# Norms of the first group in two parts of its tokens, U loaded by SP, and the first piece of w1 issued earlier

## The chip, the cores and the metric

The kernel runs on one core of a Trainium2 chip. The metric is the device time of one execution in microseconds. Runs of the same kernel are compared by their medians.

## The reference, cut to what matters

Attention with normalized queries and keys comes first, and a mixer with a two-layer network on its output second. There are 8 batches, 12 heads, 448 tokens and 64 columns a head, so the model width is 768; U is 448 x 32, V is 32 x 448, w_ch1 is 768 x 3072 and w_ch2 is 3072 x 768.

```python
def rmsnorm(x, g):
    return x / np.sqrt(np.mean(x * x, axis=-1, keepdims=True) + 1e-06) * g
q_n, k_n = rmsnorm(q, g_q), rmsnorm(k, g_k)
scores = q_n @ k_n.transpose(0, 1, 3, 2) / 8
attn = softmax(scores)
x = (attn @ v)                      # heads side by side: 8 x 448 x 768
u = x + (x.transpose(0, 2, 1) @ U @ V).transpose(0, 2, 1)
out = u + np.maximum(u @ w_ch1, 0.0) @ w_ch2
```

## The kernel before

**Groups and pairs.** The heads are worked in groups of four, three groups a batch, 24 in all, numbered gi. A group's q, k and v lie in SBUF in float32 tiles (`qf`, `kf`, `vf`, three buffers each). A partition of `qf` holds seven tokens (j) of two heads (c), 14 blocks of 64 columns. A group has two pairs of heads; a pair is scored at once, with `kz` as the stationary operand, which holds the two heads' keys with zeros beside them.

**A group's way.** `squares` (L122 to 130) squares q or k on ACT or POOL; `sums` (L133) adds each block on DVE; `roots` (L139, L140) makes 1/rms on ACT with Ln and Exp; `scale` (L143) multiplies by it on POOL or DVE and writes bf16 (`qn`, `kp`); `turn` (L311) transposes seven blocks on PE; `take_q` (L318 or L320) copies q out of PSUM and multiplies by the product of gains `gg`, on ACT or DVE; `take_k` (L326 to L328) copies k into `kz` on DVE. `values` (L170, L172) casts v on POOL into `va` and `vl`. Then `Sc` (L365, L366) does the scores of a pair in four rounds: two matmuls (one in the last round) and one exponential on ACT. `V` (L378 to L386) multiplies by the values on PE, and DVE divides and writes the batch's rows `x`. Groups from number 6 on are transposed by DMA instead.

**The gains.** g_q and g_k are loaded into one row (`grow`, tile `ob`); POOL multiplies them (L642); `prep_gains` (L232 to L237) makes a bound for the exponent on DVE and spreads both over the partitions with two PE products into `pg`, and DVE copies that into `gg` (L650). `gg` is needed by `take_q` and, as the bias, by every exponential.

**The mixer and the network.** For batch 0, `mix_t0` (L414 to L418) multiplies x by U (in `Uz`), and `mix` (L424 to L431) by V (in `Vm`, prepared on POOL by `prep_v`, L282 and L284) and adds x; this gives `uT`. `up` (L466, L468) and `down` (L479, L487) are the two layers, with weights `w1b` and `w2b` in bf16, loaded and cast by POOL's DMA queue in four and eight pieces (`load_w1` L247, `load_w2` L255).

**What sets the order.** The order is written by hand, and each engine does its instructions in the order in which the program makes them. Up to the end of batch 0's attention the list `att` holds the rounds of `Sc` and, after each, what the table `extra` names for that pair and round. After that two lists, `att` and `mlp`, are merged by costs and due times. In front of all stand the start: memsets, the loads of groups 0 to 2, the WARM matmuls on an identity (L208) that PE does before its first real work, and the norms of group 0. The last lines ahead of the merge are these:

```python
for i in range(2):
    squares(0, i)
...
sums(0, 0)
roots(0, 0, 1)
scale(0, 0, nc.gpsimd)
sums(0, 1)
roots(0, 1, 2)
pg = prep_gains()
scale(0, 1, nc.vector)
nc.vector.tensor_copy(gg, pg)
```

**Queues.** SP issues nearly all loads (L92 for q and k, L99 and L103 for v in four transfers a group, L274 for V). ACT issues k of group 0 and the two gains (L191). POOL issues U (L266 to L268, cast to bf16 under way) and the weights.

Of the kernel before, what the change touches and what calls it, by code (L numbers as in the profile page):

```python
# [13 lines left out]
ALU = AluOpType  # L14
# [3 lines left out]
WARM = 115  # L18
# [6 lines left out]
def kernel(  # L25
# [67 lines left out]

    def load_v(gi, eng=None):
# [28 lines left out]
    def squares(gi, i, eng=None, sq=None):  # L123
# [3 lines left out]
        if eng is None:  # L127
            nc.scalar.activation(sq, staged[gi][i], AF.Square)  # L128
        else:
            eng.tensor_mul(sq, staged[gi][i], staged[gi][i])  # L130

# [53 lines left out]
    grow = small[0:1, 0:2 * D].rearrange("o (i d) -> o i d", i=2)  # L185
    for gi in range(3):
        stage_tiles(gi)
    load_qk(0, 0)
    load_qk(0, 1, nc.scalar)
# [9 lines left out]

    nc.scalar.preload_act_table_set("natural_log_exp_and_others")  # L200
# [12 lines left out]
    nc.vector.memset(eps, 1e-6)  # L213
    for va, vl in zip(va_bufs, vl_bufs):
# [4 lines left out]
    for t in kz_bufs:  # L219
        for a in range(2):  # L220
            nc.vector.memset(t[D:P, a, :S], 0.0)
            nc.vector.memset(t[0:D, a, S:], 0.0)
# [3 lines left out]
    gp = small[0:1, 2 * D:4 * D + 1]  # L226
    ones = small[0:1, 4 * D + 1:4 * D + 1 + P]
    nc.vector.memset(ones, 1.0)
# [34 lines left out]
    nc.gpsimd.memset(Ub[:, NJ:, :], 0.0)  # L263
    Urows = moe_U.rearrange("(p j) r -> p j r", j=NT)
    for i in range(2):
        nc.gpsimd.dma_start(Ub[i * R:(i + 1) * R, :NJ, :], Urows[:, i * NJ:(i + 1) * NJ, :])  # L266
    nc.gpsimd.dma_start(Ub[R:P, NJ, :], Urows[:, 2 * NJ, :])
    nc.gpsimd.dma_start(Ub[0:R, NJ + 1, :], Urows[:, 2 * NJ, :])  # L268
# [4 lines left out]
    for m in range(NQ):  # L273
        nc.sync.dma_start(Vf[m * rank:(m + 1) * rank, :], moe_V)  # L274
# [12 lines left out]
    first = xp.tile([P, NW, dm], BF16, name="x", tag="x")  # L287
    Uz = first[:, 0, :NW * P].rearrange("p (j r) -> p j r", r=P)
    tz = first[:, 1, :]
    nc.gpsimd.memset(Uz, 0.0)  # L290

    def prep_u():
        nc.vector.tensor_copy(Uz[:, :, :rank], Ub[:, :NW, :])

    tb_bufs = [consts.tile([P, 2 * P], BF16, name=f"tb{i}") for i in range(2)]
    for t in tb_bufs:
        nc.gpsimd.memset(t, 0.0)
# [222 lines left out]
    def turns(gi):  # L520
# [4 lines left out]
        (0, 1): scales(1) + [(0, squares, (2, 1, pool)), (0, keep_busy, (8,))],  # L525
        (0, 2): [(0, keep_busy, (8,))],
        (0, 3): [(0, keep_busy, (8,))],
        (1, 1): [V2(0, 0)],
        (1, 2): [(0, sums, (2, 0))] + turns(1),
        (1, 3): [V2(0, 1), (0, sums, (2, 1)), (0, take_k, (1, 1)), (0, values, (1,)), (0, load, (4,)),  # L530
                 (0, weights, (1,))],
        (2, 1): scales(2) + [(0, weights, (1,)), V2(1, 0)],
# [106 lines left out]
    for i in range(2):  # L639
        squares(0, i)  # L640
    for e in range(2):
# [100 lines left out]
```

## Time and profile before

| what | value |
|---|---|
| median of 3 runs | 606.08 us (605.55 to 606.76) |
| the profiled execution's own time | 602.04 us |
| its span, first to last instruction | 600.3 us |
| busy share: PE, weight loads, DVE, ACT, POOL | 98%, 60%, 34%, 52%, 26% |
| first square of group 0 (ACT) | 5.68 us |
| scaling of q of group 0 (POOL), of k (DVE) | from 8.42, from 9.37 us |
| first exponential | 12.74 us |
| first exponential of group 1, of group 2 | 21.20 us, 29.00 us |
| first w1 issue | 21.67 us |
| first `up` matmul | 41.12 us |

Times inside the execution count from the first instruction. PE, DVE, ACT, POOL and SP are the engines; PEld is PE's loading of stationary operands, beside its matmuls. A line such as L143 is a line of the kernel before. In rows of instructions in order of time, the brackets at the end give how long the engine was idle before and what ended that. POOL's and DVE's instructions are timed one by one; rows with x2 or more merge neighbours of a kind. The granted clock of PE is given as 1.00 throughout.

### The profile page before, as it was taken

The page shows a single profiled execution, that of the slowest core. Times are in us where ns is not written, and L with a number is a line of the kernel's source. Part 1 is how long each engine was busy: PE and PEld are TensorE (multiplying, and loading weights), DVE is VectorE, ACT ScalarE, POOL GpSimd, SP SyncE. Part 2 cuts the span into 40 slices and gives each one's busy share as a digit, 9 for nine tenths or more (in the row PEclk, how much of TensorE's full clock was granted, in tenths as well). Part 3 has the DMA queues.
Part 4 walks back from the last instruction along what each step waited for, and adds up shares of the span by engine and source line. Part 5 has one row for each costly group of instructions (what it writes and reads, how often), then busy time and mean ns, then how long its engine had stood idle before and what let it go on. Part 6 is the DMA issues. An engine that isn't in the chain of part 4 may idle for free.

```text
span 600.3 us, 11625 instructions
## 1 busy us (share of the span) xinstructions
PE 586.2 (98%) x4807; PEld 357.9 (60%) x4807; DVE 206.6 (34%) x474; ACT 312.5 (52%) x479; POOL 158.5 (26%) x271
## 2 busy tenths in 40 slices
PE   8889999999999999999999999999999999999996
PEld 8555656655666556655566655665566655655563
DVE  6686535511343322531235321541234310320011
ACT  6857873477453776356744477346763344004300
POOL 7997633123213303303303312302312000000000
PEclk9999999999999999999999999999999999999999
DMA  9999996784295454675256746277305310230022
GB/s 257 221 243 246 242 199 160 149 204 96 53 206 107 132 124 113 112 179 123 48 134 99 189 116 139 58 174 169 50 2 89 84 27 0 54 72 2 0 54 52
DMA packets 118360, 71.70 MB, mean 119 GB/s; under 512 B 80420, under 2 KB 115108, under 8 KB 118308
## 3 DMA queue, kind: packets, MB, share of 16 engines
q1 hardware_dynamic: 108304, 61.04, 45.0%
q0 software_dynamic: 9728, 9.47, 9.5%
q8 instruction: 37, 0.61, 0.4%
q10 hardware_dynamic: 276, 0.46, 0.2%
q14 instruction: 15, 0.12, 0.1%
HBM read 52.20 MB, written 11.01 MB: 105 GB/s over the span
## 4 chain that ended last, share of the span: by engine, by line
PE 92%; DVE 3%; ACT 2%; DMA 1%; POOL 1%; issue 0%; POOLq 0%; DVEq 0%; ACTq 0%
PE po L479 36%; PE ph L466 35%; PE sc L365 9%; PE pv L382 5%; PE pm L451 2%; PE pv L378 1%; PE busy L208 1%; ACT E L366 1%; DMA qT<-qn 1%; DVE ssq L133 1%; PE pu L399 1%; PE pt L311 1%; DVE x L386 0%; DVE kz L326 0%; POOL sq L130 0%
## 5 line engine op out<-in xcount | busy, mean ns | idle before, releaser
L479 PE MATMUL po<-w2b,hT 128*128 128x384 bf16 x1344 | 241.6, 326 | 1.0 <-DVE x L386 1.0
L466 PE MATMUL ph<-uT,w1b 128*128 128x448 bf16 x1152 | 237.1, 352 | 0.0
L366 ACT ACTIVATE E<-sc,gg 128x896 bf16<-128x896 f32 x192 | 171.9, 911 | 75.3 <-PE sc L365 75.1
L479 PEld LDWEIGHTS <-hT 128*128 128x128 bf16 x1344 | 126.9, 98 | 79.2 <-DVE x L386 1.1
L466 PEld LDWEIGHTS <-w1b 128*128 128x128 bf16 x1152 | 109.7, 98 | 96.1
L468 ACT ACTIVATE hT<-ph 128x448 bf16<-128x448 f32 x192 | 104.0, 545 | 116.7 <-PE ph L466 114.6
L162 POOL TENSOR_TENSOR qn<-qf,rs 128x384 bf16<-128x384 f32 x36 | 29.9, 830 | 279.1 <-ACT rs L140 225.4
L365 PE MATMUL sc<-qT,kz 128*128 128x448 bf16 x336 | 93.7, 352 | 5.2 <-ACT E L366 3.5
L385 DVE RECIPROCAL r<-pv 128x4 f32<-128x4 f32 x96 | 17.4, 181 | 212.2 <-PE pv L382 211.7
L382 PE MATMUL pv<-va,E 128*128 128x65 bf16 x1152 | 57.2, 194 | 0.0
L487 DVE TENSOR_TENSOR ob<-po,x 128x384 f32<-128x384 f32 x48 | 26.8, 558 | 84.6 <-PE po L479 83.4
L382 PEld LDWEIGHTS <-E 128*128 128x128 bf16 x1152 | 50.5, 98 | 7.5
L133 DVE TENSOR_REDUCE ssq<-sq 128x14 f32<-128x896 f32 x47 | 48.8, 1076 | 2.2 <-ACT sq L128 1.7
L365 PEld LDWEIGHTS <-kz 128*128 128x128 bf16 x336 | 31.8, 98 | 29.1 <-issue 4.7
L378 PE MATMUL pv<-vl,E 128*128 128x130 bf16 x192 | 42.1, 219 | 0.0
L386 DVE TENSOR_TENSOR x<-pv,r 128x256 bf16<-128x256 f32 x96 | 40.8, 425 | 3.3
L139 ACT ACTIVATE rs<-ssq,eps 128x28 f32<-128x28 f32 (+1 forms) x25 | 7.9, 318 | 52.4 <-DVE ssq L133 41.1
L456 DVE TENSOR_TENSOR x<-pm,x 128x384 bf16<-128x384 f32 x48 | 26.6, 554 | 17.9 <-PE pm L451 16.8
L162 POOL TENSOR_TENSOR kp<-kf,rs 128x384 bf16<-128x384 f32 x36 | 29.9, 829 | 0.0
L378 PEld LDWEIGHTS <-E 128*128 128x128 bf16 x192 | 18.7, 97 | 8.1 <-issue 1.2
L170 POOL CAST va<-vf 128x768 bf16<-128x768 f32 x24 | 20.7, 863 | 2.0 <-DMA vf<-in_v_dram 2.0
L128 ACT ACTIVATE sq<-qf 128x896 f32<-128x896 f32 x20 | 18.8, 942 | 2.3 <-DMA qf<-in_q_dram 2.3
(84 smaller groups left out, 265.2 us busy)
## 6 DMA issues: line engine op xcount, KB each, us to landing
qf<-in_q_dram SPq DMA_DIRECT2D x24, 448.0 KB, 4.2
kf<-in_k_dram SPq DMA_DIRECT2D x23, 448.0 KB, 5.5
out_dram<-ob SPq DMA_DIRECT2D x50, 192.0 KB, 2.7
vf<-in_v_dram SPq DMA_DIRECT2D x48, 192.0 KB, 5.4
w1b<-in_moe_w_ch_dram POOLq DMA_DIRECT2D x4, 1152.0 KB, 17.1
w2b<-in_moe_w_ch_dram POOLq DMA_DIRECT2D x8, 576.0 KB, 17.5
vf<-in_v_dram SPq DMA_DIRECT2D x48, 32.0 KB, 4.9
out_dram<-ob SPq DMA_DIRECT2D x12, 96.0 KB, 2.5
```

What stands on the lines that cost most here:

```text
L133: nc.vector.tensor_reduce(ssqs[gi][:, i, :], sqs.pop((gi, i)), AX, ALU.add)
L162: nc.gpsimd.tensor_tensor(main.rearrange("p (t i) d -> p i t d", i=2), src[:, c, :2 * NJ].rearrange("p (i t) d -> p i t d", i=2), rs[:, c, ...
L365: nc.tensor.matmul(sc[:, i, :S], kz[:, c:c + P], qT, start=True, stop=True)
L366: nc.scalar.activation(es[(b, pr)][:, 2 * r:2 * r + n, :], sc[:, :n, :S], AF.Exp, scale=scal, bias=bias)
L378: nc.tensor.matmul(pv[:, i].rearrange("p e d -> p (e d)"), E[:, NJ, w:w + P], vl[:, lp, :], start=True, stop=False)
L382: nc.tensor.matmul(pv[:, i, e, :], E[:, e * (NJ + 1) + j, w:w + P], va[:, (lp + 2 * e) * NJ + j, :], start=False, stop=(e == 1 and j == NJ ...
L386: nc.vector.tensor_tensor(xs[b].rearrange("p i (h d) -> p i h d", d=D)[:, 2 * half:2 * half + 2, h0:h0 + 3:2, :], pv[:, :, :, :D], r.rearr ...
L456: nc.vector.tensor_tensor(dst, ph[lo:hi], x[lo:hi], ALU.add)
L466: nc.tensor.matmul(ph, w1b[:, dt, ht * P:(ht + 1) * P], uT[:, dt, off:off + S], start=(dt == 0), stop=(dt == KD - 1))
L468: nc.scalar.activation(hT[:, ht, off:off + S], ph, AF.Relu)
L479: nc.tensor.matmul(po, hT[:, ht, col:col + P], w2b[:, ht, half * HALF:(half + 1) * HALF], start=(ht == 0), stop=(ht == KH - 1))
L487: nc.vector.tensor_tensor(ob[:, h], po, urows(b, col, half), ALU.add)
```

## The change

The loads of q and k of group 0 are split by tokens into j = 0 to 3 and j = 4 to 6, and all four go into SP's queue, q first. Squares, sums and scalings of group 0 are done by the same parts. WARM goes from 115 to 62, and ten more of these matmuls follow the gain products. ACT loads its function table ahead of issuing the gains. The product of the gains stands on POOL ahead of the memset of Vm, and the copy of `gg` stands ahead of k's scaling on DVE. Half of the kz memsets go from DVE to POOL. U is loaded by SP in float32 (into a free part of an x buffer) and cast by DVE in `prep_u`; V is one transfer from a repeated source instead of four. The memsets of Uz and tb go behind the scalings of group 0, and the first piece of w1 is issued right after them; the other pieces of w1 move up by one place. The second square of group 1 goes behind `take_q`, the values of group 0 behind a square of group 2. In `extra`, the scalings of group 1 go one round later, q's turn of group 1 ahead of k's by a round, and the sum of q of group 2 into the start.

```diff
@@ -15,7 +15,7 @@
 
 EXP_ROOM = 80.0
 EXP_SHIFT = 60.0
-WARM = 115
+WARM = 62
 ROWS_FROM = 1
 DMA_FROM = 6
 LEAD = 1.8
@@ -91,6 +91,15 @@
         src = (q, k)[i][b, h0:h0 + n].rearrange("(c a) (p j) d -> (a p) c (j d)", a=2, j=NT)
         (eng or nc.sync).dma_start(staged[gi][i].rearrange("p (c j) d -> p c (j d)", c=2), src)
 
+    def load_qk_part(gi, i, lo, hi):
+
+        b, h0, n = groups[gi]
+        src = (q, k)[i][b, h0:h0 + n].rearrange("(c a) (p j) d -> (a p) c (j d)", a=2, j=NT)[:, :, lo * D:hi * D]
+        nc.sync.dma_start(by_c(staged[gi][i])[:, :, lo:hi, :].rearrange("p c j d -> p c (j d)"), src)
+
+    def by_c(t):
+        return t.rearrange("p (c j) d -> p c j d", c=2)
+
     def load_v(gi, eng=None):
         b, h0, n = groups[gi]
         t = staged[gi][2]
@@ -128,6 +137,22 @@
             nc.scalar.activation(sq, staged[gi][i], AF.Square)
         else:
             eng.tensor_mul(sq, staged[gi][i], staged[gi][i])
+
+
+    def squares_part(i, lo, hi):
+        if (0, i) not in sqs:
+            sqs[(0, i)] = normp.tile([P, 2 * NT, D], FP32, name="sq", tag="sq")
+        nc.scalar.activation(by_c(sqs[(0, i)])[:, :, lo:hi, :], by_c(staged[0][i])[:, :, lo:hi, :], AF.Square)
+
+    def sums_part(i, lo, hi):
+        nc.vector.tensor_reduce(ssqs[0][:, i, :].rearrange("p (c j) -> p c j", c=2)[:, :, lo:hi],
+                                by_c(sqs[(0, i)])[:, :, lo:hi, :], AX, ALU.add)
+
+    def scale_part(i, lo, hi, eng):
+        eng.tensor_tensor(
+            normed[0][i].rearrange("p j c d -> p c j d")[:, :, lo:hi, :], by_c(staged[0][i])[:, :, lo:hi, :],
+            rss[0][:, i].rearrange("p (c j) -> p c j ()", c=2)[:, :, lo:hi, :].to_broadcast([P, 2, hi - lo, D]),
+            ALU.mult)
 
     def sums(gi, i):
         nc.vector.tensor_reduce(ssqs[gi][:, i, :], sqs.pop((gi, i)), AX, ALU.add)
@@ -183,10 +208,15 @@
 
     small = outp.tile([P, dm], FP32, name="ob", tag="ob")
     grow = small[0:1, 0:2 * D].rearrange("o (i d) -> o i d", i=2)
+    gp = small[0:1, 2 * D:4 * D + 1]
+    ones = small[0:1, 4 * D + 1:4 * D + 1 + P]
     for gi in range(3):
         stage_tiles(gi)
-    load_qk(0, 0)
-    load_qk(0, 1, nc.scalar)
+    PARTS = ((0, 4), (4, NT))
+    for i in range(2):
+        for lo, hi in PARTS:
+            load_qk_part(0, i, lo, hi)
+    nc.scalar.preload_act_table_set("natural_log_exp_and_others")
     for i, g in enumerate((g_q, g_k)):
         nc.scalar.dma_start(grow[:, i, :], g.rearrange("(o d) -> o d", o=1))
     for i in range(2):
@@ -197,8 +227,6 @@
     load_v(1)
     load_v(2)
 
-    nc.scalar.preload_act_table_set("natural_log_exp_and_others")
-
     ident = consts.tile([P, P], BF16)
     make_identity(nc, ident)
 
@@ -211,21 +239,21 @@
 
     eps = consts.tile([P, 1], FP32)
     nc.vector.memset(eps, 1e-6)
+    nc.vector.memset(ones, 1.0)
     for va, vl in zip(va_bufs, vl_bufs):
         nc.vector.memset(va[:, :, D:D1], 1.0)
         nc.vector.memset(vl, 0.0)
         for e in range(2):
             nc.vector.memset(vl[e * R:(e + 1) * R, :, e * D1 + D:(e + 1) * D1], 1.0)
-    for t in kz_bufs:
+    for t, eng in zip(kz_bufs, (nc.vector, nc.gpsimd)):
         for a in range(2):
-            nc.vector.memset(t[D:P, a, :S], 0.0)
-            nc.vector.memset(t[0:D, a, S:], 0.0)
+            eng.memset(t[D:P, a, :S], 0.0)
+            eng.memset(t[0:D, a, S:], 0.0)
+    for e in range(2):
+        nc.gpsimd.tensor_mul(gp[:, e * D:(e + 1) * D], grow[:, 0, :], grow[:, 1, :])
 
     gg = consts.tile([P, 2], FP32)
     bias = gg[:, 1:2]
-    gp = small[0:1, 2 * D:4 * D + 1]
-    ones = small[0:1, 4 * D + 1:4 * D + 1 + P]
-    nc.vector.memset(ones, 1.0)
 
     def prep_gains():
         m = gp[:, P:]
@@ -260,18 +288,19 @@
 
 
     Ub = consts.tile([P, NJ + 2, rank], BF16)
-    nc.gpsimd.memset(Ub[:, NJ:, :], 0.0)
+    first = xp.tile([P, NW, dm], BF16, name="x", tag="x")
+    Uf = first[:, 2, :2 * (NJ + 2) * rank].bitcast(FP32).rearrange("p (j r) -> p j r", r=rank)
+    nc.gpsimd.memset(Uf[:, NJ:, :], 0.0)
     Urows = moe_U.rearrange("(p j) r -> p j r", j=NT)
     for i in range(2):
-        nc.gpsimd.dma_start(Ub[i * R:(i + 1) * R, :NJ, :], Urows[:, i * NJ:(i + 1) * NJ, :])
-    nc.gpsimd.dma_start(Ub[R:P, NJ, :], Urows[:, 2 * NJ, :])
-    nc.gpsimd.dma_start(Ub[0:R, NJ + 1, :], Urows[:, 2 * NJ, :])
+        nc.sync.dma_start(Uf[i * R:(i + 1) * R, :NJ, :], Urows[:, i * NJ:(i + 1) * NJ, :])
+    nc.sync.dma_start(Uf[R:P, NJ, :], Urows[:, 2 * NJ, :])
+    nc.sync.dma_start(Uf[0:R, NJ + 1, :], Urows[:, 2 * NJ, :])
 
     NQ = P // rank
     Vf = outp.tile([P, dm], FP32, name="ob", tag="ob")[:, :S]
     Vm = consts.tile([P, NQ, S + R], BF16)
-    for m in range(NQ):
-        nc.sync.dma_start(Vf[m * rank:(m + 1) * rank, :], moe_V)
+    nc.sync.dma_start(Vf, moe_V.rearrange("(m r) s -> m r s", m=1).to_broadcast([NQ, rank, S]))
 
     nc.gpsimd.memset(Vm, 0.0)
 
@@ -284,17 +313,19 @@
             nc.gpsimd.tensor_copy(Vm[r, m, SM:S], cols[:, 2 * NJ])
 
 
-    first = xp.tile([P, NW, dm], BF16, name="x", tag="x")
     Uz = first[:, 0, :NW * P].rearrange("p (j r) -> p j r", r=P)
     tz = first[:, 1, :]
-    nc.gpsimd.memset(Uz, 0.0)
 
     def prep_u():
-        nc.vector.tensor_copy(Uz[:, :, :rank], Ub[:, :NW, :])
+        nc.vector.tensor_copy(Ub, Uf)
+        nc.vector.tensor_copy(Uz[:, :, :rank], Uf[:, :NW, :])
 
     tb_bufs = [consts.tile([P, 2 * P], BF16, name=f"tb{i}") for i in range(2)]
-    for t in tb_bufs:
-        nc.gpsimd.memset(t, 0.0)
+
+    def fill_mixer():
+        nc.gpsimd.memset(Uz, 0.0)
+        for t in tb_bufs:
+            nc.gpsimd.memset(t, 0.0)
 
 
     qk, es, xs = {}, {}, {}
@@ -522,14 +553,14 @@
 
     extra = {
         (0, 0): [(0, keep_busy, (8,))],
-        (0, 1): scales(1) + [(0, squares, (2, 1, pool)), (0, keep_busy, (8,))],
-        (0, 2): [(0, keep_busy, (8,))],
+        (0, 1): [(0, keep_busy, (8,))],
+        (0, 2): scales(1) + [(0, squares, (2, 1, pool)), (0, keep_busy, (8,))],
         (0, 3): [(0, keep_busy, (8,))],
         (1, 1): [V2(0, 0)],
-        (1, 2): [(0, sums, (2, 0))] + turns(1),
-        (1, 3): [V2(0, 1), (0, sums, (2, 1)), (0, take_k, (1, 1)), (0, values, (1,)), (0, load, (4,)),
-                 (0, weights, (1,))],
-        (2, 1): scales(2) + [(0, weights, (1,)), V2(1, 0)],
+        (1, 2): [(0.4, turn, (1, 0)), (0, take_q, (1, 0)), (0, take_q, (1, 1))],
+        (1, 3): [(0.4, turn, (1, 1)), (0, take_k, (1, 0)), V2(0, 1), (0, take_k, (1, 1)), (0, sums, (2, 1)),
+                 (0, values, (1,)), (0, load, (4,)), (0, weights, (1,))],
+        (2, 1): scales(2) + [V2(1, 0)],
         (2, 3): [V2(1, 1)],
         (3, 1): [V2(2, 0)],
         (3, 2): turns(2),
@@ -637,30 +668,37 @@
                 mlp.append((0.98, down, (b, col, half, part, 4), b))
 
     for i in range(2):
-        squares(0, i)
-    for e in range(2):
-        nc.gpsimd.tensor_mul(gp[:, e * D:(e + 1) * D], grow[:, 0, :], grow[:, 1, :])
-    sums(0, 0)
+        for part in PARTS:
+            squares_part(i, *part)
+    for part in PARTS:
+        sums_part(0, *part)
     roots(0, 0, 1)
-    scale(0, 0, nc.gpsimd)
-    sums(0, 1)
+    for part in PARTS:
+        scale_part(0, *part, nc.gpsimd)
+    for part in PARTS:
+        sums_part(1, *part)
     roots(0, 1, 2)
     pg = prep_gains()
-    scale(0, 1, nc.vector)
+    keep_busy(10)
     nc.vector.tensor_copy(gg, pg)
+    for part in PARTS:
+        scale_part(1, *part, nc.vector)
     squares(1, 0)
-    squares(1, 1)
-    values(0)
+    fill_mixer()
+    weights(1)
     squares(2, 0, nc.gpsimd,
             uT.rearrange("p k c -> p (k c)")[:, :4 * NT * D].bitcast(FP32).rearrange("p (j d) -> p j d", d=D))
+    values(0)
     turn(0, 0)
     take_q(0, 0, True)
     take_q(0, 1, True)
+    squares(1, 1)
     turn(0, 1)
     take_k(0, 0)
     sums(1, 0)
     sums(1, 1)
     take_k(0, 1)
+    sums(2, 0)
     load(3)
 
     ia = im = 0
```

## The prediction

> **What bounds the kernel now.** I read the table of stretches first, then the start in order of time on each engine, then the transfers from issue to landing, then the chain that ended last from 28 to 42 us. In the table the columns are length, busy time of PE, its weight loads, DVE, ACT and POOL, granted clock, DMA share and GB/s.
>
> ```profile
> 0.00:12.74 12.74, 10.89 (x139) 10.37 (x140) 8.27 (x33) 6.96 (x11) 8.84 (x19) 1.00 0.92 264
> 12.74:29.00 16.26, 13.61 (x174) 9.42 (x172) 11.73 (x31) 14.44 (x21) 14.72 (x16) 1.00 0.98 218
> 29.00:41.10 12.10, 9.72 (x134) 6.62 (x133) 10.36 (x25) 7.91 (x12) 11.25 (x15) 1.00 1.14 237
> 41.10:600.30 559.20, 552.01 (x4370) 331.54 (x4367) 176.26 (x387) 283.22 (x437) 123.67 (x222) 1.00 0.52 111
> ```
>
> From 41.10 us, the first `up` matmul, PE is busy 552.01 of 559.20 us and has one order of work. The change does not touch that order, so what it does is how far it moves the 41.10. Before that point PE is full of fillers and no engine is full: it is a chain. Its first half, in order of time (start, duration, what, and in brackets the idle time before it):
>
> ```profile
> 5.68 0.95 ACT L128 ACTIVATE sq<-qf 128x896 f32<-128x896 f32 x1 [2.26 <-DMA qf<-in_q_dram]
> 6.54 0.93 ACT L128 ACTIVATE sq<-kf 128x896 f32<-128x896 f32 x1
> 6.56 0.60 POOL L642 TENSOR_TENSOR ob<-ob 1x64 f32<-1x64 f32 x2
> 7.79 0.31 ACT L139 ACTIVATE rs<-ssq,eps 128x14 f32<-128x14 f32 x1 [0.31 <-DVE ssq L133]
> 8.42 1.69 POOL L143 TENSOR_TENSOR qn<-qf,rs 128x896 bf16<-128x896 f32 x1 [1.27 <-ACT rs L140]
> 9.37 1.69 DVE L143 TENSOR_TENSOR kp<-kf,rs 128x896 bf16<-128x896 f32 x1 [0.15 <-ACT rs L140]
> 11.72 0.38 DVE L326 COPY kz<-pt 64x448 bf16<-64x448 bf16 x1 [0.59 <-PE pt L311]
> 12.74 1.91 ACT L366 ACTIVATE E<-sc,gg 128x896 bf16<-128x896 f32 x2 [0.32 <-PE sc L365]
> 17.04 1.69 POOL L143 TENSOR_TENSOR kp<-kf,rs 128x896 bf16<-128x896 f32 x1
> 21.20 1.91 ACT L366 ACTIVATE E<-sc,gg 128x896 bf16<-128x896 f32 x2 [0.99 <-PE sc L365]
> 21.67 0.90 POOL L247 DMA_DIRECT2D w1b<-in_moe_w_ch_dram  x1
> 25.37 1.68 POOL L143 TENSOR_TENSOR kp<-kf,rs 128x896 bf16<-128x896 f32 x1
> 29.00 3.33 ACT L366 ACTIVATE E<-sc,gg 128x896 bf16<-128x896 f32 x4 [0.47 <-PE sc L365]
> 33.00 1.09 DVE L133 TENSOR_REDUCE ssq<-sq 128x14 f32<-128x896 f32 x1 [0.49 <-POOL sq L130]
> ```
>
> The reader is to see three links. The loads of group 0 start the squares at 5.68; norms, scaling and turns give the first exponential at 12.74. The scaling of group 1 on POOL ends at 18.73 and its first exponential comes at 21.20, after a stall of 0.99; that of group 2 ends at 27.05 and its exponential comes at 29.00. Then POOL's squares of group 3 hold DVE's sum (0.49), which stands ahead of the mixer's copy.
>
> **The change, link by link.** Every time here is an estimate from the rows named.
>
> Loads. The table by half microseconds has 262 KB moved by 3.3 us, 459 by 3.9, 721 by 4.5 and 917 by 5.0; the q and k of group 0 (917 KB) landed at 5.64 and 5.94, 0.65 to 0.95 later. In one queue the four parts then land near 4.1, 4.7, 5.3 and 5.9. Their shorter runs (1024 and 768 bytes against 1792) and four issues of 0.5 us in one queue could make the last one 0.3 later; two queues less could make it as much sooner. I take 5.95.
>
> Squares. By the exponential's rows (1.01 us for 896, 0.65 for 448) ACT spends 0.80 ns an element, so a last part of 384 takes 0.53. It ends at 6.48 instead of 7.47; the sums of q are done by then, and Ln and Exp (0.52 together) give q's roots at 7.0, against 8.34. k's last sum (about 0.5, at 6.6) ends at 7.1 and its roots at 7.65.
>
> POOL before its scaling. Four U issues (2.3 us) go, and the memsets of Uz and tb (1.1) move behind; four kz memsets of 448 come (0.4 each by the 256 and 512 rows) and end by 3.0. Then the product of gains waits for g_q and g_k, which ACT now issues after its table load: 0.74 + 1.28 + 0.60 puts the second at 2.65. **Their landing is not in the trace.** From below, V's 56 KB took 1.9 us in a quiet stretch; from above, the product ran at 6.56 without a wait, so at most 4.7. I take 1.9, the nearer by queue and kind: 4.55, plus the product (0.55), a small memset and Vm's 1.85 makes 7.0, just when the roots come. At 4.7 it is 9.75.
>
> Scaling. POOL's two parts cost 1.05 + 0.83 by the rows of 896 (1.69) and 384 (0.83): 7.05 to 8.9. DVE has prep_gains (0.55), now followed by the copy of gg, which waits for PE's two gain products; behind it in DVE's queue stand both k parts, and the turns of k wait for those. PE's 62 fillers: the trace has 43 started by 5.9 us (106 ns each) and 56 ns each after about 6.4, so the 62nd ends near 7.2; products 7.7 to 8.3, gg at 8.5, ten fillers to 8.9. The k parts run from 8.9 to 9.85. In the rows, DVE's 1.69 from 9.37 ends at 11.06, which is 0.95 after POOL's ended at 10.11. So I price it at 0.95 once POOL is through.
>
> The Trainium skill (SBUF — State Buffer, "SBUF: two separate sides") has it that a VectorE operation with two SBUF inputs and a GpSimd one that reads SBUF take a shared port in turn, each for its whole length. The trace agrees, here and at 41.86, where DVE's same operation took 1.95 and ended 0.94 after POOL's. Without that rule DVE's 1.69 would be its own length, and the k parts would end at 10.25.
>
> First exponential. k's last three turns instead of seven end 0.35 after 9.85; kz's copy at 10.25 (was 11.72), scores at 10.7. ACT turns q at 9.55 to 10.7 and now has one square (0.93) ahead of the exponential: 11.5, **1.25 sooner**.
>
> Group 1. Eight exponentials and the roots took 7.48 us, so ACT is through at 18.9. POOL: fills (1.1) to 10.0, w1's issue (0.9) to 10.9, squares to 12.6, values of group 0 to 14.2, scaling with the roots of 14.5 to 17.9 (was 18.73). Since q's turn and copies and the sum of group 2 now stand ahead of it, only k's turn and copy follow: 1.6 us instead of 2.47. Exponential at 19.5, **1.7 sooner**.
>
> Group 2. POOL squares to 19.55, values of group 1 (1.4), w1's second piece (0.9), scaling 3.35. With v in time the scaling starts at 22.1 and ends 1.6 sooner. But the first w1 piece is now in flight from about 12, when k and v of groups 2 and 1 still are. The transfers show what that costs (KB, us from issue to landing):
>
> ```profile
> qf<-in_q_dram SPq DMA_DIRECT2D x1, 448.0 KB, 8.1
> w1b<-in_moe_w_ch_dram POOLq DMA_DIRECT2D x1, 1152.0 KB, 12.5
> qf<-in_q_dram SPq DMA_DIRECT2D x1, 448.0 KB, 9.0
> kf<-in_k_dram SPq DMA_DIRECT2D x1, 448.0 KB, 11.0
> ```
>
> The first is group 2's, the others were in flight together at 22 us and later, when the engines moved about 250 GB/s. If w1 takes half, SP has 125; about 950 KB of group 2's k and group 1's v remain at 12, so v lands near 20.0 to 20.3 (was 16.9). Values to 21.7, w1 to 22.6, scaling to 25.95: **1.1 sooner** instead of 1.6. If w1 gets most, v lands at 21.9 and the scaling ends at 27.6, 0.5 later. I take 1.1.
>
> Mixer. One w1 issue less (0.9) stands between that scaling and POOL's squares of group 3, which end about 2 us sooner; DVE's sum no longer waits (0.49) and the mixer's copy follows with 0.45 gained. Against it, prep_u has one copy more on DVE, each free to sit behind a POOL instruction as the 1.01 us for 128 columns at 30.29 did: 0 to 0.5. I take 0.4. U (four issues) and V (one instead of four) on SP put off the loads of group 3 by some 3 us; they landed by 24.1 for squares at 31.28, so that is covered; without cover it would cost its 3 us less the 2.
>
> Sum: 1.1 + 0.4 = 1.5 us. The profiled execution goes from 602.04 (span 600.3, 1.74 around it) to 600.5; it lies 4.0 under the median of the runs, 606.08. Against that I forecast 604.6.
>
> **Rivals.**
> (a) Nothing is shared: v in time, all 1.6 + 0.45, and a little more where stalls close: 603.6. The idle DMA of 16 to 20 us (106 to 117 GB/s) speaks for it, the three rows above against it.
> (b) w1 in the way: values of groups 0 and 1 late, 0.2 to 0.9 gained: 605.5. Half of the DMA time after 21 us speaks for it.
> (c) **The gains, slower.** g's transfers queue behind the loads and hold POOL. At 4.7 us POOL scales at 9.75 instead of 8.42, q and k end 1.5 later, the first exponential is at 14.3, group 1's scaling at 20.6, group 2's at 27.9: 0.85 later, 606.9. It decides from about 4.0 us of landing; between 3.0 and 4.0 the gain shrinks to under 1. For it: U's 4 to 12 KB took 5.6 to 6.0 us at that time, though in POOL's queue. Against it: ACT's ring is otherwise empty.
> (d) PE is slow again after 62 fillers: two score matmuls and eight fillers then take 1.4 us at 106 ns per 128 columns, against 0.83 of the exponential, four times: 2.3 lost, 606.9. My gaps of PE are under 1 us, and gaps of 0.8 at 15.5 slowed nothing.
> The Trainium skill (TensorE: Matmul & The Clock Gate, "What's actually happening") gives an idle window of about 3.4 us for that; no gap forecast here reaches it, so by the rule (d) does not happen.
> (e) The parts are not independent: each load waits for the one before, and k's last lands near 11 instead of 5.94: 610. The four v loads of one tile were issued back to back, which speaks against it.
>
> **Chances.** Forecast (604.0 to 605.2) 0.46, (a) 0.13, (b) 0.20, (c) 0.14, half of it slower, (d) 0.04, (e) 0.03. A measurement of this kernel can tell about 0.2%, 1.2 us, from no change. Faster by more: 0.60; within: 0.27; slower: 0.13. The range takes in (a) with 0.3 to spare and (c): 603.3 to 606.9.
>
> **What would show it.** Right: first square near 4.2, POOL's first scaling near 7, first exponential near 11.5, those of groups 1 and 2 near 19.5 and 27.9, `up` near 39.6. Wrong: POOL idle before the gains' product past 5.5 (c), values of group 1 waiting for v past 20.5 (b), fillers back at 106 ns (d). The forecast falls if PE idles more after 41 us than the 7.2 it does now.

## The result, and the profile after

The changed kernel takes **608.73 us** (median of 6 runs, 607.94 to 609.72) against 605.55 (603.45 to 606.76) for the kernel before on the same chip: a ratio of 1.0053, 95% interval 1.0036 to 1.0070. It is slower; 604.6 was forecast. Its profiled execution took 607.94 us (span 606.2), that of before 602.04 (span 600.3).

The table of stretches of the changed kernel, with the columns that the prediction names and bounds at the same events:

```profile
0.00:13.78 13.78, 9.06 (x95) 7.79 (x96) 7.85 (x32) 7.20 (x14) 9.39 (x21) 0.94 0.86 235
13.78:31.39 17.61, 14.46 (x174) 9.89 (x173) 11.70 (x31) 14.48 (x20) 14.11 (x16) 0.95 0.97 188
31.39:47.58 16.19, 11.27 (x135) 7.47 (x133) 10.65 (x26) 7.98 (x12) 11.05 (x14) 0.89 1.13 245
47.58:606.20 558.62, 552.00 (x4370) 331.54 (x4367) 176.25 (x387) 283.19 (x437) 123.61 (x222) 1.00 0.51 110
```

The last row is what it was (552.00 busy us of PE; 552.01 before). The three ahead of it, to the first `up`, are 1.04, 1.35 and 4.09 us longer. The instructions in order of time, of the same kernel:

```profile
3.67 1.06 ACT L145 ACTIVATE sq<-qf 128x512 f32<-128x512 f32 x2 [1.65 <-DMA qf<-in_q_dram]
7.44 1.08 ACT L145 ACTIVATE sq<-kf 128x512 f32<-128x512 f32 x2 [2.70 <-DMA kf<-in_k_dram]
9.05 1.84 POOL L152 TENSOR_TENSOR qn<-qf,rs 128x512 bf16<-128x512 f32 x2 [2.91 <-ACT rs L165]
9.77 0.38 PE L265 MATMUL pg<-ob 1*128 1x1 f32 x2 [2.59 <-DVE ob L262]
13.53 1.06 PE L236 MATMUL busy<-ident 128*128 128x128 bf16 x8
13.78 1.01 ACT L397 ACTIVATE E<-sc,gg 128x896 bf16<-128x896 f32 x1 [0.46 <-PE sc L396]
23.05 1.91 ACT L397 ACTIVATE E<-sc,gg 128x896 bf16<-128x896 f32 x2 [1.47 <-PE sc L396]
32.58 0.86 POOL L311 CAST Vm<-ob 32x384 bf16<-32x384 f32 x1 [1.71 <-DMA ob<-in_moe_V_dram]
36.24 1.67 POOL L139 TENSOR_TENSOR sq<-qf 128x896 f32<-128x896 f32 x1 [1.70 <-DMA qf<-in_q_dram]
37.94 1.09 DVE L158 TENSOR_REDUCE ssq<-sq 128x14 f32<-128x896 f32 x1 [2.94 <-POOL sq L139]
38.88 1.68 POOL L139 TENSOR_TENSOR sq<-kf 128x896 f32<-128x896 f32 x1 [0.98 <-DMA kf<-in_k_dram]
39.68 0.56 PE L455 MATMUL ph<-Vm,x 128*128 128x448 bf16 x1 [3.17 <-DVE x L449]
```

Two places stand out. At the start q's parts are there at 3.67, but k's only at 7.44 (5.94 before). ACT does k's squares ahead of q's roots, so POOL scales at 9.05 instead of 8.42; PE has used up its 62 fillers and is idle for 2.59 us, and fillers then take 1.06 us for eight, where they take 0.61 at full clock. In the mixer, POOL waits for V (1.71), then for q and k of group 3 (1.70 and 0.98); DVE's sum waits for POOL (2.94), the mixer's copy stands behind that sum (38.94, before 34.01), and PE waits for the copy (3.17). SP's queue says why (start, length of the issue, what; the first two rows are of the kernel before, the others of the changed one):

```profile
15.84 2.12 SPq L274 DMA_DIRECT2D ob<-in_moe_V_dram  x4
18.07 0.39 SPq L92 DMA_DIRECT2D qf<-in_q_dram  x1
```

```profile
18.02 1.24 SPq L296 DMA_DIRECT2D x<-in_moe_U_dram  x2
20.21 0.47 SPq L297 DMA_DIRECT2D x<-in_moe_U_dram  x1
21.44 0.47 SPq L298 DMA_DIRECT2D x<-in_moe_U_dram  x1
24.32 0.67 SPq L303 DMA_DIRECT2D ob<-in_moe_V_dram  x1
25.49 0.38 SPq L92 DMA_DIRECT2D qf<-in_q_dram  x1
```

U's issues are not back to back: in the waits of that queue each stands until an earlier load has landed (0.9, 0.7, and 2.4 us ahead of V). The semaphores in the trace say which: the loads of SP and ACT use eight semaphores in turn, so an issue waits until the load eight places ahead of it has landed. U's last two issues, at 20.21 and 21.44, follow the landing of v's loads of 13.06 and 13.95 (7.1 and 7.5 us after their issue), though these fill other buffers; four small transfers of U take four of the eight places. Group 3's q goes out at 25.49 instead of 18.07. Meanwhile the DMA engines have almost nothing to do (last columns: clock, DMA share, GB/s):

```profile
24.50:25.00 0.50, 0.15 (x1) 0.00 (x0) 0.50 (x1) 0.46 (x1) 0.50 (x1) 1.00 0.07 18
25.00:25.50 0.50, 0.49 (x10) 0.40 (x9) 0.47 (x2) 0.04 (x1) 0.13 (x1) 1.00 0.07 18
```

### The profile page after: what moved, and what is told of

Its sections match the earlier page's. It is cut to its first block, busy times and chain, and to the rows that moved or that the text cites. A ratio compares the mean times of both kernels' runs of the same rounds, so it can differ in the third digit from the quotient of the medians.

```text
span 606.2 us, 11544 instructions
## 1 busy us (share of the span) xinstructions
PE 586.8 (97%) x4764; PEld 356.7 (59%) x4764; DVE 206.5 (34%) x474; ACT 312.9 (52%) x481; POOL 158.2 (26%) x272
## 4 chain that ended last, share of the span: by engine, by line
PE 89%; DMA 6%; DVE 2%; SPq 1%; ACT 1%; issue 0%; POOL 0%; POOLq 0%; DVEq 0%
PE po L510 35%; PE ph L497 35%; PE sc L396 9%; PE pv L413 5%; DMA vf<-in_v_dram 3%; DMA qf<-in_q_dram 2%; PE pm L482 2%; PE pv L409 1%; DMA qT<-qn 1%; PE pu L430 1%; DVE ssq L158 1%; ACT E L397 0%; PE pt L342 0%; DVE x L417 0%; SPq L98 0%; PE ph L455 0%
## 5 line engine op out<-in xcount | busy, mean ns | idle before, releaser
L396 PE MATMUL sc<-qT,kz 128*128 128x448 bf16 x336 | 95.0, 356 | 4.9 <-ACT E L397 3.8
L158 DVE TENSOR_REDUCE ssq<-sq 128x14 f32<-128x896 f32 x45 | 46.7, 1076 | 3.0 <-POOL sq L139 2.9
L417 DVE TENSOR_TENSOR x<-pv,r 128x256 bf16<-128x256 f32 x96 | 40.7, 424 | 3.3
L518 DVE TENSOR_TENSOR ob<-po,u_rest 128x384 f32<-128x384 f32 x8 | 4.5, 558 | 45.1 <-PE po L510 45.1
```

What stands on the lines that cost most here:

```text
L158: nc.vector.tensor_reduce(ssqs[gi][:, i, :], sqs.pop((gi, i)), AX, ALU.add)
L396: nc.tensor.matmul(sc[:, i, :S], kz[:, c:c + P], qT, start=True, stop=True)
L417: nc.vector.tensor_tensor(xs[b].rearrange("p i (h d) -> p i h d", d=D)[:, 2 * half:2 * half + 2, h0:h0 + 3:2, :], pv[:, :, :, :D], r.rearr ...
L518: nc.vector.tensor_tensor(ob[:, h], po, urows(b, col, half), ALU.add)
```

## The experiments

All ratios are to the kernel before, run beside each on its chip. `up` is the start of the first `up` matmul, "MB" what the DMA had moved by 30 us and by 60 us, "wait" PE's idle time just ahead of the second tile of `down`; these four are from the profiled execution.

| run | ratio (95%) | `up` | MB by 30 / 60 | wait |
|---|---|---|---|---|
| before | 1 | 41.1 | 7.16 / 14.49 | 0.98 |
| before again (b1) | 0.9996 (0.9969 to 1.0023) | 40.5 | 7.02 / 14.35 | 3.02 |
| changed | 1.0053 (1.0036 to 1.0070) | 47.6 | 6.16 / 13.55 | 0.16 |
| changed, U by POOL (e1) | 1.0019 (1.0000 to 1.0038) | 43.7 | 7.12 / 14.38 | 0 |
| changed, w1 at its old places (e2) | 1.0112 (1.0083 to 1.0141) | 43.1 | 5.94 / 13.15 | 6.31 |
| changed, k's parts by ACT first (e3) | 1.0006 (0.9988 to 1.0024) | 44.7 | 7.42 / 14.78 | 0 |
| changed, 115 fillers (e4) | 1.0077 (1.0046 to 1.0107) | 48.7 | 6.26 / 13.51 | 0 |
| changed, V by four transfers (c2) | 1.0012 (0.9992 to 1.0031) | 45.3 | 6.40 / 14.02 | 0.57 |
| changed, e1 + c2 + k by ACT behind the gains, 74 fillers (c1) | 1.0003 (0.9987 to 1.0019) | 46.0 | 7.08 / 14.46 | 0 |
| changed, e1 + c2 + 115 fillers (c3) | 0.9997 (0.9981 to 1.0013) | 43.4 | 6.63 / 14.11 | 0 |
| c3, k by ACT first, gains by SP (f1) | 0.9991 (0.9967 to 1.0014) | 44.1 | 7.31 / 14.67 | 0 |
| f1, POOL's order of before (f2) | 0.9996 (0.9966 to 1.0025) | 42.2 | 6.82 / 14.24 | 0 |
| before, U and V by SP (b3) | 1.0072 (1.0048 to 1.0096) | 42.8 | 6.55 / 13.82 | 3.90 |
| before, V by one transfer (b5) | 1.0047 (1.0024 to 1.0070) | 40.9 | 6.77 / 14.03 | 4.72 |
| before, U by SP (b6) | 1.0060 (1.0040 to 1.0080) | 43.8 | 6.27 / 13.48 | 3.54 |
| before, k whole by SP (b4) | 1.0017 (0.9996 to 1.0038) | 42.3 | 7.13 / 14.36 | 1.07 |
| before, w1's first piece sooner (b2) | 0.9964 (0.9943 to 0.9986) | 40.1 | 7.20 / 14.59 | 0.79 |
| b2, 0.59 MB more (d2) | 1.0010 (0.9990 to 1.0030) | 40.2 | 7.40 / 14.76 | 2.56 |
| b2, w1's second piece sooner (d1) | 0.9945 (0.9924 to 0.9966) | 40.7 | 7.46 / 14.97 | 0 |

**First: which part of the change costs?** Four runs undo one part each. U by POOL again:

```diff
-        nc.sync.dma_start(Uf[i * R:(i + 1) * R, :NJ, :], Urows[:, i * NJ:(i + 1) * NJ, :])
+        nc.gpsimd.dma_start(Ub[i * R:(i + 1) * R, :NJ, :], Urows[:, i * NJ:(i + 1) * NJ, :])
...
-        nc.vector.tensor_copy(Ub, Uf)
```

> The changed kernel with U back on POOL's queue (cast under way), V still one transfer by SP. Theory Q (the end of the front is late because U's four and V's one issue stand in SP's queue behind landings of v, so that V and group 3's q and k come late): q of group 3 is issued by about 22 instead of 25.5, POOL no longer waits for V (1.7) and q of group 3 (1.7) near 32 to 36, the mixer's copy comes about 3 us sooner, and the kernel is about 3 us faster than the changed one. Theory S (all is lost at the start, by k's late landing and PE's slow clock): first exponentials and total as in the changed kernel, within 0.5 us. Theory W (w1's early piece fills the engines): U's four issues matter little, since each waits for a landing that w1 delays; under 1 us gained.

605.18 us; q of group 3 goes out at 17.10, `up` is 3.9 sooner than in the changed kernel. U by SP was the largest part of the loss, 0.34 of the 0.53%.

w1 back at its old places:

```diff
-    weights(1)
     squares(2, 0, nc.gpsimd,
...
+        (2, 1): scales(2) + [(0, weights, (1,)), V2(1, 0)],
```

> The changed kernel with the pieces of w1 at their old places. Theory W: v of groups 1 and 2 lands 4 to 6 us sooner, so SP is through with U and V by about 20 and q of group 3 is issued near 20 instead of 25.5; the waits of POOL for V and q of group 3 go, about 3 us faster than the changed kernel. Theory Q: SP's entries still wait for landings one behind the other, 1 to 2 us gained. Theory S: within 0.5 us of the changed kernel.

611.13 us, the slowest of all, though `up` comes 4.5 us **sooner** than in the changed kernel: none of U's issues waits for v now, and group 3's q goes out at 21.09. Between `up` and the end stands a wait that the forecast had no term for. DVE and PE in order of time, of this run:

```profile
99.01 0.45 DVE L372 TENSOR_SCALAR qT<-qT,gg 128x896 bf16<-128x896 bf16 x1 [10.52 <-DMA qT<-qn]
99.59 0.42 DVE L417 TENSOR_TENSOR x<-pv,r 128x256 bf16<-128x256 f32 x1
100.07 2.42 PE L510 MATMUL po<-w2b,hT 128*128 128x384 bf16 x7 [6.31 <-DVE x L417]
```

PE starts 0.06 us after the division of DVE that is named. That division stands in DVE's order behind the copy of q of group 6, and the copy had waited 10.52 us for q's transposes by DMA. SP issues these behind the front, and they move beside the last pieces of w2: the copy starts at 99.01, and the last piece of w2, issued at 75.69, lands 23.3 us later, at 99.0. That piece itself is in time, since `down` first needs it in its fourth tile, at 112.95. So w1 sooner costs the front 4.5 us here and still gains in all: bytes moved early let those transposes land sooner.

k's parts by ACT, ahead of its table load and the gains:

```diff
-            load_qk_part(0, i, lo, hi)
+            load_qk_part(0, i, lo, hi, (nc.sync, nc.scalar)[i])
```

> The changed kernel with the two k parts of group 0 issued by ACT instead of SP. Theory S1 (four parts in one queue make k land at 7.4 and 7.9): k's last part lands near 5.9, the first exponential comes near 12 instead of 13.8, PE has no gap of 2.6 us ahead of the gain products and stays at full clock to 16 us; of that 1 to 1.5 us reach the total if nothing later waits. Theory Q: the first exponential comes sooner, but q of group 3 and V land as late as before, and the total moves by under 0.5 us.

604.22 us. k's squares come at 5.94 and from 4 to 8 us the DMA moves 377 GB/s (286 in the changed kernel), but the gains now land behind the loads and hold POOL:

```profile
6.89 0.59 POOL L253 TENSOR_TENSOR ob<-ob 1x64 f32<-1x64 f32 x2 [3.53 <-DMA ob<-in_g_k_dram]
```

POOL's scaling starts at 9.28, with q's roots there at 7.41. This is the prediction's rival (c), in this run and not in the changed kernel. More fillers:

```diff
-WARM = 62
+WARM = 115
```

> The changed kernel with 115 matmuls ahead of the gain products instead of 62. Theory C (PE's gap from 7.2 to 9.8 us lets the clock fall to half from 12.4 to 15.6): full clock throughout, the gain products end some 0.4 later than 10.1, rounds of scores 0.84 apart instead of 1.6 for the first three, group 1's exponential about 1 us sooner; total 0 to 1 us faster. Theory Q: no difference in the total beyond 0.3 us, since group 3's loads set the end of the front whatever the first exponentials do.

608.78 us: the clock is full at the start, yet the first exponential stays at 13.77, because k's scaling stands behind the copy of gg, which now waits 1.50 us for PE's fillers; 0.8 us is gained up to group 2 and given back where POOL waits 5.5 us for V. The slow clock did not set the end.

**Second: the same parts put into the kernel before, one at a time.** The first run is that kernel once more, for its own spread.

> The kernel before, unchanged, for a second profile: the first one's execution took 602.04 us where the runs' median is 605.5. Theory E (the network's second layer waits at about 93 us for the last pieces of w2, which pass DMA engines that are full from 28 us on, and this wait, 0.98 us in the first profile, differs between executions): an execution of about 605 shows the same front (first up matmul at 41 to 42) and a wait of 3 to 5 us at 93. The rival, that the front itself differs: first up matmul at 44 to 45 and a wait of under 1 us.

The front is alike and the span differs by 2.7 us: 2.0 in that wait, and the matmuls behind it are slow at first (2.10 us for six; 1.14 at full clock).

```profile
94.20 2.10 PE L479 MATMUL po<-w2b,hT 128*128 128x384 bf16 x6 [3.02 <-DVE x L386]
```

So the kernel before has a second end already, and its runs differ by it. In the next three, w1's first piece is issued ahead of `values(0)`; or U and V go as in the change; or k goes whole in SP's queue.

```diff
+    weights(1)
     values(0)
...
-        (2, 1): scales(2) + [(0, weights, (1,)), V2(1, 0)],
+        (2, 1): scales(2) + [V2(1, 0)],
```

> The kernel before with the first piece of w1 issued ahead of the values of group 0 (some 10 us sooner) and not at its old place; nothing else changed. Theory E: the DMA engines' idle stretch at 16 to 20 us is used, the last piece of w2 lands sooner, the wait at 93 us goes: 1 to 3 us faster than the kernel before. Theory W (w1 in the way of v and k of groups 1 and 2): the front ends 1 to 3 us later, and the kernel is slower by 0 to 2 us.

601.70 us, faster than before: 224 GB/s instead of 114 from 16 to 20 us.

```diff
-        nc.gpsimd.dma_start(Ub[i * R:(i + 1) * R, :NJ, :], Urows[:, i * NJ:(i + 1) * NJ, :])
+        nc.sync.dma_start(Uf[i * R:(i + 1) * R, :NJ, :], Urows[:, i * NJ:(i + 1) * NJ, :])
...
-        nc.sync.dma_start(Vf[m * rank:(m + 1) * rank, :], moe_V)
+    nc.sync.dma_start(Vf, moe_V.rearrange("(m r) s -> m r s", m=1).to_broadcast([NQ, rank, S]))
```

> The kernel before with U loaded by SP in float32 and cast on DVE, and V one transfer instead of four; nothing else changed. Theory Q: SP has one issue more than before (five for eight places), each waiting for a landing of v; w1 is not in flight then, so q of group 3 is issued 0 to 2 us later than 18.07 and the total stays within 1 us of the kernel before. If the front ends over 2 us later, U and V by SP are enough by themselves; if not, it took w1's early piece or k's late landing to make them cost.

608.98 us, 43 GB/s from 16 to 20 us, `up` 1.7 later than before and a wait of 3.90 on top. Group 3's q goes out at 18.32, only 0.25 later than before: without w1's early piece the wait in SP's queue is short.

```diff
-    load_qk(0, 1, nc.scalar)
+    load_qk(0, 1)
```

> The kernel before with k of group 0 issued by SP behind q, whole, instead of by ACT. Theory S1 (one queue moves the first loads more slowly): from 4 to 8 us the engines move about 300 GB/s instead of 373, k lands 1 us or more later than 5.94 and the first exponential comes 1 us or more later than 12.74; total 0 to 1.5 us slower. The rival (the shorter runs of the parts slow the engines): whole loads in one queue move 370 GB/s as before, k lands near 6, nothing is lost.

604.74 us: 260 GB/s from 4 to 8 us instead of 373, and a cost at the edge of what can be told. The three ratios, +0.72%, +0.17% and -0.36%, add to +0.53%, which is the change's 1.0053. That it comes out so well is in part luck: U and V alone do not add (below), and the other parts of the change are not in the sum.

**Third: U or V?** V by one transfer alone, then U by SP alone (the diff above, cut in two), and V by four in the changed kernel.

> The kernel before, with V alone loaded by one transfer from the repeated source. If V's transfer is the costly half of U and V by SP (it runs on few engines, and group 3's q waits behind it in SP's queue): from 16 to 20 us the DMA moves 40 to 60 GB/s, as in the run with both (43), against 114 in before; group 3's q lands 5 us or more after its issue; `up` is 1.5 us or more later than 40.5, and the time is 606.3 to 608.5. If U is the costly half: 90 GB/s or more from 16 to 20 us, `up` within 0.7 of 40.5, 603.5 to 605.

> The kernel before, with U alone loaded by SP in full precision and cast by VectorE; V stays four transfers. If U is the costly half (its two casts from full precision take 2.8 us of VectorE beside POOL where the one in before took 1.0, and its four issues stand ahead of V and q in SP's queue): `up` 1.5 us or more later than 40.5, 606.3 to 608.5. If V is the costly half: the casts are seen again (2 to 3 us), but `up` is within 1 us of 40.5 and the time 604 to 605.5. If the two need each other, both this run and the one with V alone stay under 605.5, while the run with both was 608.98.

> The changed kernel, with V by four transfers again; U stays with SP in full precision. If V's single transfer is the costly half: from 24 to 26 us the DMA moves over 100 GB/s (31 in the changed kernel), V's first cast on POOL starts before 31 instead of 32.58, `up` is 2 us or more before 47.6, and the time is 605 to 607. If U is: within 1 us of the changed kernel, 607.7 to 609.5.

608.15, 608.67 and 606.15 us. My reading that V's transfer made the hole at 16 to 20 us was wrong: with V alone it moves 115 GB/s there, as before, with U alone 43. U's four issues, 2.6 us, stand ahead of V and q in SP's queue. U also costs at the front, where its second cast runs into POOL's square of 31.60 to 33.29 and takes 1.79 us, after a cast of 1.05, against one copy of 1.01 before (0.32 in the changed kernel, where no square runs beside it):

```profile
31.59 1.79 DVE L295 CAST x<-x 128x128 bf16<-128x128 f32 x1
```

V by one transfer leaves `up` at 40.9 and costs all of its 2.8 us in that wait: by 60 us the DMA has moved 14.03 MB instead of 14.35 to 14.49. Each costs, and together (+0.72%) less than the sum (+1.07%).

**Fourth: is that wait a matter of supply?** If so, a dose of useless bytes must cost its own time, and bytes sooner must gain. d2 loads the first piece of w2 twice; d1 moves the second piece of w1 from (1, 3) to (1, 1).

```diff
     weights(1)
+    load_w2(0, 4, 0)
     values(0)
```

> The kernel before with the first piece of w1 ahead of the first values, and behind it one transfer more of 0.59 MB that nothing needs (the first piece of w2, loaded a second time at its own place). If the DMA's supply is the second end: 0.59 MB at 245 GB/s is 2.4 us, all of it as a longer wait for w2 before `down` (0.79 in the run without it), and the time is 603 to 605.5 against 601.7. If w2 comes when it is issued, and the supply has room: 601 to 602.5.

```diff
-        (1, 1): [V2(0, 0)],
+        (1, 1): [V2(0, 0), (0, weights, (1,))],
```

> The kernel before with the first piece of w1 ahead of the first values (as in the run that was 601.7) and the second piece sooner as well, near 16 us instead of 21. If what the DMA has moved by 30 us sets when the last of w2 lands: more than 7.2 MB by 30 us, no wait for w2 left, `up` near 40 and the time 599.5 to 601.5. If a piece sooner only takes bandwidth from q, k and v that the front waits for: `up` 1 us or more after 40.1, 602 to 604.

Both as the supply has it, though what PE waits for is the copy behind q's transposes and not w2: in all eleven runs with a wait, PE goes on 1.06 us after that copy starts. The dose leaves `up` at 40.2, makes the wait 2.56 instead of 0.79, and costs 0.46%, 2.8 us; 0.59 MB at 245 GB/s are 2.4. With two pieces sooner the wait is gone and so is most of the spread (600.61 to 601.70 in 6 runs; b2 600.57 to 604.76 in 12). **d1 is the fastest version: 601.43 us, 0.9945 of before**; it has none of the norms in parts.

**Fifth: what do the norms in parts do by themselves?** Four versions of the changed kernel, freed of its known costs.

```diff
-    for i in range(2):
-        for lo, hi in PARTS:
-            load_qk_part(0, i, lo, hi)
+    for lo, hi in PARTS:
+        load_qk_part(0, 0, lo, hi, nc.sync)
...
+    for lo, hi in PARTS:
+        load_qk_part(0, 1, lo, hi, nc.scalar)
...
-WARM = 62
+WARM = 74
```

> The changed kernel without its three suspected costs: k's parts issued by ACT behind the gains (q's stay with SP), U by POOL and V in four transfers as in before, and 12 more fillers for the clock; w1 stays sooner. If the costs found so far simply add, the clock is full from 10 us, the first exponential near 11.5 (12.74 in before), `up` at 39 to 40.5 and the time 599 to 601.5, below both kernels. If the end is set by w2's arrival alone, an earlier front is given back at the second pass: `up` at 39 to 40.5, a wait of over 3 us before `down`, 602 to 604. If k's parts on ACT's queue push the gains or the squares back as they did when they stood ahead of the gains (gains at 6.89): first exponential after 13 and the time over 603.

605.50 us. The sum was not reached: k behind the gains lands at 7.3 and 9.1, the clock is 0.50 from 12 to 18 us and the first exponential comes at 15.03. c3 leaves the parts in one queue and has the fillers of before:

> The changed kernel with U by POOL, V by four transfers and 115 fillers as in before: what is left of the change is the parts in one queue, the new order and w1 sooner. If U and V cost 0.5 to 0.7%, as they do alone, and the clock the rest: full clock throughout, `up` at 42 to 43.5, no wait for w2, 600.5 to 602.5. If the late k (about 7.4 us) and the order around it cost by themselves: first exponential at 12.7 or later, `up` at 43.5 to 45.5 and 603 to 605.5.

603.95 us, no faster than before although w1 is sooner. The copy of gg waits 0.99 us for PE's fillers and k's scaling waits behind it (first exponential 13.45), and the second sum of group 2, which now stands behind group 1's last copies of k (DVE at 23.21; in b2 at 21.24, ahead of them), holds ACT for 0.50. PE then idles for 1.13 us, and after that the clock is halved:

```profile
24.00:26.00 2.00, 0.87 (x16) 0.65 (x15) 1.42 (x5) 1.64 (x4) 0.96 (x2) 1.00 0.74 94
26.00:28.00 2.00, 2.00 (x17) 1.27 (x16) 0.00 (x0) 1.65 (x3) 2.00 (x2) 0.50 1.13 201
```

f1 gives the parts two queues, with the gains behind q's parts on SP; f2 then puts the gains' product behind U's issues and Vm's memset, as before:

```diff
-            load_qk_part(0, i, lo, hi)
+            load_qk_part(0, i, lo, hi, eng)
...
-        nc.scalar.dma_start(grow[:, i, :], g.rearrange("(o d) -> o d", o=1))
+        nc.sync.dma_start(grow[:, i, :], g.rearrange("(o d) -> o d", o=1))
```

> The changed kernel with U by POOL, V by four transfers and 115 fillers, and the parts in two queues: k's by ACT as its first instructions, the gains by SP behind q's parts. If the one queue is what is left of the loss (k at 7.4 us instead of 5.9): k's squares near 6, POOL's first scaling near 7.5, first exponential 11.8 to 12.3, `up` at 40.5 to 42, 600 to 602. If it is the new order of the work around group 1 and 2: first exponential as early, but the gap of PE and the half clock near 25 us stay, `up` at 42.5 to 43.5 and 602.5 to 604. If parts cost more than they save: first exponential at 12.7 or later.

```diff
-    for t, eng in zip(kz_bufs, (nc.vector, nc.gpsimd)):
+    for t, eng in zip(kz_bufs, (nc.vector, nc.vector)):
...
-    for e in range(2):
-        nc.gpsimd.tensor_mul(gp[:, e * D:(e + 1) * D], grow[:, 0, :], grow[:, 1, :])
```

> The run with the parts in two queues, and POOL's order of before: all memsets of kz on VectorE, the gains' product behind U's issues and Vm's memset instead of ahead of them. There POOL waited to 6.14 for the gains and then did U and Vm until 10.88, 2.5 us after q's roots (7.65). If that order was the cost: scaling of q at 7.7 to 8, first exponential 11.8 to 12.5 (15.77 there, 12.40 in the kernel before with w1 sooner), `up` at 40 to 41, 600 to 602. If the later order (group 1's turns and sums) costs as well: `up` at 41 to 42.5, 601.5 to 603.5. If the parts gained what was forecast of them (1.25 us at the first exponential): 11.5 or sooner.

604.42 and 603.41 us. In f1 the gains land at 6.14, POOL does U and Vm behind them and scales at 10.78, with the roots there at 7.65. In f2 nothing holds POOL up:

```profile
5.70 0.52 ACT L145 ACTIVATE sq<-qf 128x384 f32<-128x384 f32 x1 [0.53 <-DMA qf<-in_q_dram]
7.68 1.83 POOL L152 TENSOR_TENSOR qn<-qf,rs 128x512 bf16<-128x512 f32 x2 [0.59 <-ACT rs L165]
9.97 0.16 DVE L682 COPY gg<-pg 128x2 f32<-128x2 f32 x1 [1.59 <-PE pg L263]
```

q's second part lands at 5.70, where the whole q was there at 5.02 in b2 and 5.68 in before. The scaling starts at 7.68; in b2, d1, d2 and before it was 7.75, 7.92, 8.10 and 8.42. At their best the parts gain 0.1 to 0.7 us at that link, not the 1.3 of the forecast (roots at 7.0 instead of 8.34). The earliest scaling of q of all runs, 7.03, is that of b4, with whole loads and k behind q in one queue. Then the copy of gg, which the change puts ahead of k's scaling, waits for PE's fillers: k is scaled from 10.06, in b2 from 8.70.

## Why the prediction was wrong, point by point

**The step that failed most** is in "Mixer": U and V on SP "put off the loads of group 3 by some 3 us ... so that is covered". They were put off by 7.4 (25.49 against 18.07), since I counted the issues and not what each waits for in its queue, and the cover was gone: V's, q's and k's waits on POOL. Of the 7.4, 2.2 were there before U's first issue (18.02; before, V's first stood at 15.84), and from U to q it took 7.47 instead of 2.23. U and V alone do not make that: it is 3.53 in b3, and 3.35 in e2, where w1's early piece is missing. What U's and V's issues wait for is v, and v's loads share the DMA with that piece. From group 2's exponential to `up` I forecast 11.7 us (27.9 to 39.6); it took 16.19. With U on POOL (e1) it is 12.9.

**The frame** was incomplete: "what it does is how far it moves the 41.10". That is right only while nothing later waits, and before has a wait of 0.98 at 92.80, 3.02 in another execution. The share of the DMA that I had for 41 to 600 us, 0.52, is a mean. The part of that stretch that counts, of the kernel before, has 1.18, and the copy that waits there, and PE behind it, are these:

```profile
60.00:100.00 40.00, 38.41 (x358) 23.69 (x357) 18.70 (x43) 26.80 (x43) 19.45 (x30) 1.00 1.18 221
```

```profile
91.74 0.45 DVE L341 TENSOR_SCALAR qT<-qT,gg 128x896 bf16<-128x896 bf16 x1 [5.18 <-DMA qT<-qn]
92.80 4.07 PE L479 MATMUL po<-w2b,hT 128*128 128x384 bf16 x24 [0.98 <-DVE x L386]
```

So the end is the later of two: the front, and q's transposes of group 6, which land with the last of w2 and so come later by what the DMA has not moved by then. In the changed kernel they nearly meet: `up` at 47.58 decides, with a wait of only 0.16. My test, PE idle over 7.2 us after 41, would not have found it (558.62 less 552.00 is 6.6). For the same reason the price of w1's early piece had the wrong sign: I took 0.5 us lost; alone it gains 0.36%, and in the changed kernel it puts `up` off by 4.5 us and still gains 2.4 (e2).

**Loads**: q's parts landed near 3.67, sooner than 4.1 and 4.7; k's at about 7.4 and 7.95 instead of 5.3 and 5.9. One queue does not move what two do: 286 against 373 GB/s from 4 to 8 us, and 260 with whole loads in one queue (b4), so it is the queue and not the parts. Over all runs it is 260 to 312 where q and k stand in one queue and 341 to 397 in two (c1, with k behind the gains, 284). k's landing varies: with the four parts in one queue its first square came at 5.67 to 7.44 in six executions, and the changed kernel's is the latest.

**Squares and Scaling** followed from k, whose squares stand ahead of q's roots on ACT: the roots were due at 7.0 and stand in POOL's wait to 9.05. First exponential 13.78 against 11.5.

**POOL before its scaling** was right in kind: the gains came at 3.73 (forecast 2.65 + 1.9), and rival (c) did not occur in the changed kernel. It did in e3 and f1, where two queues of loads run beside the gains.

**Rival (d)**, at 0.04, occurred: the granted clock was 0.57, 0.50, 0.50 and 0.72 in the four microseconds from 12. The gaps were not "under 1 us" because k was late. It cost little by itself (e4).

**Group 1 and Group 2** gained nothing on the way: from first exponential to group 1's 9.27 us (before 8.46), to group 2's 8.34 (before 7.80), the first with the slow clock, the second with ACT's 0.50 for the sum that c3 shows. **(a) and (e)** were not what happened: SP's queue waits between loads, but not between the four parts. Of **(b)**, w1 was in v's way, yet it showed in U's issues and not in the values.

## What to carry to other kernels

Look for a second end before pricing the first: cut a long stretch until a wait or a full DMA share shows, and count the bytes that must be through by then; here a MB not moved early came back as 3 to 6 us (a dose of 0.59 MB made the wait 1.8 longer; 1.44 MB less by 60 us, from b2 to e2, put off the second tile of `down` from 91.6 to 100.1, with `up` 2.9 later as well). Follow a wait further back than the instruction it names: DVE's division came just before PE, but had itself stood behind a copy that waited for a transfer. A load that is moved to another queue is priced by what stands ahead of it and behind it there, with the waits of each, not by its issue time; where completion semaphores are used in turn, as here, a small transfer takes a place as a large one does. Work cut into parts pays only if the last part is there sooner.

## What the runs showed of the hardware

A slow clock does not need a long gap. In the changed kernel PE was idle for 2.59 us to 9.77 and busy 1.96 of the 4 us from 8, and the clock was 0.57 in 12 to 13 us. In c3 a gap of 1.13 us (0.87 busy of 2) was followed by 0.50; in f2 the same stretch (0.87 of 2) was followed by 1.00. The Trainium skill (TensorE: Matmul & The Clock Gate, "What's actually happening") asks for an idle window of some 3.4 us that runs freely of the kernel. That it runs freely agrees with c3 against f2. But PE was wholly idle for so long in none of the three, so on the length the measurement decides: a stretch that was half busy was enough, twice in three.

With V by a single transfer and nothing else changed (b5) the DMA share fell to 0.03 and 7 GB/s at 18.0 to 18.5 us, where the kernel before has 0.43 and 104. The Trainium skill (DMA: Bandwidth & Descriptors, "Rules for kernel authors") says that a repeated source with c copies in front keeps a transfer on at most c of the 16 engines; V has 4 copies. The low share would fit that, but no run here counts the engines, and the changed kernel's 0.07 does not show it: with V by four (c2) the share there falls to 0.29 and 67 GB/s at 24.0 to 24.5 too. b5 gives the price here, 2.8 us, none of it at the instruction that uses V.

What stays open: U's two costs, the queue and the casts, were seen in the rows of b6 but not parted. An order on DVE with that division ahead of the copy of group 6, which would take PE's second end away from the transposes, was not run, and neither were loads with more than eight semaphores. Most figures of the front are of one execution a version.
